# Joining the halves of 32-step inverses: two heads to a 32-row tile instead of four tiles to 64 rows

## The chip, the core and the metric

The kernel runs on one core of a Trainium2 chip. The metric is device time in microseconds (us) of one execution. The engines are TensorE (PE, with PEld for its weight loads), VectorE (DVE), ScalarE (ACT), GpSimd (POOL) and SyncE (SP), which issues every DMA of this kernel. A matrix product reads its two operands from SBUF (`lhsT` is loaded as weights, `rhs` streams past them) and writes PSUM, which here is eight banks of 128 partitions by 512 floats.

## The reference

Four sequences of 768 steps with 8 heads of width 40 carry a 40x40 state through a decayed delta rule; the outputs of the heads, side by side, then go through a normalised two-layer feed-forward network of width 1280 with a residual:

```python
for t in range(S):
    y[:, :, t] = np.einsum('bhd,bhde->bhe', rt, state)
    Sa = np.einsum('bhde,bhe->bhd', state, at)
    state_decay = state * wt[:, :, None, :] - np.einsum('bhd,bhe->bhde', Sa, bt)
    state = state_decay + np.einsum('bhd,bhe->bhde', vt, kt)
...
xn = (x - mu) / np.sqrt(var + 1e-06) * g_ln
ch = np.maximum(xn @ w_ch1, 0.0) @ w_ch2
return (x + ch)
```

Everything is float32.

## The kernel before

**Chunks.** The 768 steps are cut into 24 chunks of C = 32 steps, and the 32 pairs of sequence and head (called heads below) are worked on together. Inside a chunk the rule needs, for each head, the inverse of a 32x32 unit lower triangular matrix made of the decayed keys. The inverse is built from halves of B = 16 steps: with L21 the lower left block of the matrix, W11 and W22 are the inverses of the two diagonal blocks, and the whole inverse has W11 and W22 on its diagonal and W22 L21 W11 below (signs are in L).

**The functions of a chunk.** `prep` (running products of the decays on DVE, scaled operands on POOL, the triangular matrices by the product of L376, from there to DRAM as `d_l`); `invert` (16x16 inverses by elimination, 28 small operations for each slab of two chunks, on DVE for chunks 0 and 1 and on POOL from chunk 2 on; results to DRAM as `d_h`, whose rows hold L21, W11 and the transposed W22 side by side, 16 columns each); `merge`, which this change rewrites; `chain` (the products that need the state: L513, then L523, which multiplies by the joined inverse `tt`, then the new state by L538); `post` (outputs of the chunk: turns L571 and L583, products L598 and L615); `norm` and `moe` (the feed-forward network, once for every two chunks: first layer L786, relu to `hh` on ACT in L789, the rest `hl` on DVE in L791, second layer L770).

**`merge` before.** The 32 heads lie in four groups of eight, two to each half of 64 partitions. Tile `hv` has for each group 32 rows: of these, only the lower 16 are loaded, and constant identities and zeros, written once at the start (L304 to L315), stand around the loaded blocks. Four DMAs a chunk load it, two of them cut into pieces of 16 floats. A product L456 takes `hv` 64 rows by 64 columns against 32 columns (16 of them a chunk: eight for each half), ACT copies the result into `qm` (L458), a second product of the same shape multiplies `qm` with blocks of `hv` (L466), and ACT copies that to `tt` (L468).

**Who sets the order.** Every operation is handed to a planner (`Plan`) with its engine, an estimated duration, a key (about the chunk in which it is due) and what it reads and writes. `Plan.order` plays the whole program through with these estimates and writes out one fixed order for each engine; on the chip each engine runs its list in that order. On PE the planner alternates: products of the recurrence (called sparse here: small tiles) until 2.9 us of them have run, then feed-forward products (dense) for 1.7 us, since it counts instruction records of PE and assumes that 128 of them need 3.8 us to be fetched. PSUM banks 0 to 3 (group A) serve the sparse products, 4 and 5 the first layer, 6 and 7 the second; an operation that opens a bank takes the first that is free in the plan. When the recurrence has ended, the dense products that are left run alone.

Of the kernel before, what the change touches and what calls it, by code (L numbers as in the profile page):

```python
# [16 lines left out]
ALU = mybir.AluOpType  # L17
# [4 lines left out]
C = 32  # L22
B = C // 2
D = 40
# [158 lines left out]
def body(ctx, tc, ea, eb, vr, rd, vt, w1, w1x_in, w2, gl, fe, fd, out):  # L183
    nc = tc.nc
# [27 lines left out]
    start = ring(2, "start", 16, 33)  # L212
# [12 lines left out]
    hv = ring(2, "hv", 8, 9 * B)  # L225
    qm, = ring(1, "qm", 8, 4 * B)
    tt = ring(2, "tt", 8, C)
# [38 lines left out]
    def consts():  # L266
# [21 lines left out]
        op("POOL", 0.3, -84, (), ["qm"], lambda: G.memset(qm, 0.0))  # L288
# [12 lines left out]
        op("ACT", 0.3, -95, (), [("small", 0)], lambda: (A.memzero(small[0]["sd"]), A.sqrt(small[0]["sd"], small[0]["sd"])))  # L301
        for i in range(2):
            j = i + 1
            op("POOL", 0.8, -85 + i, (), two("hv", i, 4), lambda i=i: G.memset(hv[i], 0.0))  # L304

            def f(i=i):
                for q, qs in enumerate(QUADS):
                    up, lo = (ident[qs, 32 * q + B * x:32 * q + B * x + B].unsqueeze(1).broadcast_to([32, 8, B])
                              for x in range(2))
                    at = slice(2 * B * (q % 2), 2 * B * (q % 2) + B)  # L310
                    A.copy(out=hv[i][qs, :, at], in_=lo)
                    A.copy(out=hv[i][qs, :, 6 * B:7 * B], in_=up)
                    if i == 0:
                        A.copy(out=qm[qs, :, at], in_=lo)
            op("ACT", 2.6 if i == 0 else 1.8, -50 + i, ["ident"], two("hv", i, 4) + (["qm"] if i == 0 else []), f)  # L315
# [121 lines left out]
    def merge(c):  # L437
# [3 lines left out]
        for q in range(4):  # L441
            m = 32 * j + 8 * q
            to = hv[i][32 * q + B:32 * q + C]
            to = to[:, :, 3 * B:6 * B] if q % 2 else to.rearrange("a h (x y) -> a h x y", x=3)[:, :, :, B:2 * B]
            of = d_h[s][:, m:m + 8]
            dma(c - 1.3 - soon(c), 55 if q % 2 else 110, [("d_h", s, 0), ("d_h", s, 1)], [("hv", i, q)], to,
                of if q % 2 else of.rearrange("a h (x t) -> a h x t", x=3), 0.5)
        blocks = lambda t, a: t.rearrange("p h (x t) -> p h x t", t=B)[:, :, a:a + 3:2]
        halves = [slice(64 * bb, 64 * bb + 64) for bb in range(2)]
        b = Bank("A")  # L450

        def f(b=b):
# [538 lines left out]
```

## Time and profile before

| what | value |
|---|---|
| three runs | 588.72, 589.93, 594.56 us; median 589.93 |
| the profiled execution | 585.58 us, of it 583.4 us from first to last instruction |
| PE busy | 523.4 us, 90% |
| DVE, ACT, POOL busy | 404.7, 312.3, 279.8 us (69, 54, 48%) |
| the two products of `merge` (L456, L466) | 28.6 and 28.7 us busy, 768 records each |
| the product that uses `tt` (L523) | 20.5 us busy, 1536 records |
| PE granted clock, mean | 0.963 |

A float32 product has two records in the trace, a turn (transpose by the identity) one, a float32r product (feed-forward) one. Records of PE overlap and their ends are modelled, so what a group of products costs is read from its start to the start of the next group, not from the sum of its durations. Some matmuls run at half the granted clock early in the program; from 125 us on it is full.

### The profile page before, as it was taken

The numbers are of one execution on the slowest core, as the hardware profiler recorded it, in microseconds if no ns is written. First come the engines' busy times: TensorE is split into PE (matmuls) and PEld (weight loads), VectorE is DVE, ScalarE is ACT, GpSimd is POOL, SyncE is SP. The second block draws the span as 40 slices with busy tenths as digits, with TensorE's granted clock in tenths as the row PEclk, the third lists the DMA queues.
The fourth block names the chain that finished last, engine by engine and source line by source line (L and its number), as shares of the span: only waits on it lengthen the run. The fifth ranks groups of instructions, "written<-read, shape, count | busy, mean of one in ns | idle before, by whom it ended". The sixth has DMA issues, their size and how long they took to land.

```text
span 583.4 us, 30518 instructions
## 1 busy us (share of the span) xinstructions
PE 523.4 (90%) x13366; PEld 478.0 (82%) x13366; DVE 404.7 (69%) x872; ACT 312.3 (54%) x770; POOL 279.8 (48%) x510
## 2 busy tenths in 40 slices
PE   2528886799999999999999999999999999899995
PEld 2417675699999899998999899999998888799895
DVE  7984977868868668587585774783875648667522
ACT  8536457556555555665555547555746554565221
POOL 9515335575377573753845818637728408000000
PEclk9999558799999999999999999999999999999999
DMA  5374655534444533445444434344452444522000
GB/s 170 76 196 130 180 131 147 145 102 101 118 108 94 134 83 84 128 94 125 109 112 115 107 89 111 92 129 92 106 117 74 92 121 116 126 76 85 5 24 27
DMA packets 103146, 62.32 MB, mean 107 GB/s; under 512 B 82144, under 2 KB 88288, under 8 KB 103008
## 3 DMA queue, kind: packets, MB, share of 16 engines
q1 hardware_dynamic: 103008, 60.32, 41.3%
q8 instruction: 106, 1.74, 1.3%
q14 instruction: 32, 0.26, 0.2%
HBM read 48.49 MB, written 9.44 MB: 99 GB/s over the span
## 4 chain that ended last, share of the span: by engine, by line
PE 82%; DVE 6%; DMA 4%; issue 4%; ACT 2%; POOL 1%; SPq 1%; DVEq 0%; POOLq 0%; ACTq 0%
PE bank L770 20%; PE bank L786 19%; PE bank L466 4%; PE bank L456 4%; PE bank L598 4%; PE bank L376 4%; PE bank L523 3%; PE bank L538 3%; PE bank L615 3%; PE bank L513 3%; PE bank L583 3%; PE bank L488 3%; PE bank L571 2%; PE bank L709 2%; PE bank L398 2%
## 5 line engine op out<-in xcount | busy, mean ns | idle before, releaser
L770 PE MATMUL bank<-w,hh 128*128 128x320 f32 x480 | 114.9, 324 | 0.3 <-issue 0.3
L786 PE MATMUL bank<-xh,w 128*128 128x256 f32 x480 | 107.3, 287 | 1.3 <-issue 0.9
L791 DVE SCALAR_TENSOR_TENSOR hl<-bank,hh 128x256 fp32r<-128x256 f32 x120 | 50.3, 420 | 76.6 <-ACT hh L789 73.8
L789 ACT ACTIVATE hh<-bank 128x256 fp32r<-128x256 f32 x120 | 46.1, 384 | 102.8 <-PE bank L786 100.8
L786 PEld LDWEIGHTS bank<-xh,w 128*128 128x128 f32 x480 | 82.1, 189 | 3.1 <-issue 1.3
L770 PEld LDWEIGHTS bank<-w,hh 128*128 128x128 f32 x480 | 76.4, 188 | 3.4 <-issue 0.4
L770 PE MATMUL bank<-w,hl 128*128 128x320 f32 x240 | 73.8, 307 | 0.0
L359 POOL TENSOR_TENSOR x2s<-wa,qE 40x512 f32<-40x512 f32 x44 | 57.8, 1314 | 23.1 <-DVE qE L347 16.0
L786 PE MATMUL bank<-xl,w 128*128 128x256 f32 x240 | 67.2, 280 | 0.0
L366 POOL TENSOR_TENSOR bk<-bk,gE 104x1024 f32<-104x1024 f32 x22 | 51.5, 2342 | 31.6 <-DMA bk<-in_eb_dram 15.5
L498 POOL MEMSET x5s<- 64x512 f32 x48 | 25.1, 522 | 82.1 <-PE bank L615 66.9
L430 POOL TENSOR_TENSOR yv<-yv,ytmp 64x28 f32<-64x28 f32 (+6 forms) x154 | 53.7, 349 | 12.1
L426 POOL TENSOR_TENSOR ytmp<-yv 64x28 f32<-64x28 f32 (+6 forms) x154 | 51.7, 335 | 11.4
L493 ACT COPY xk<-bank 64x320 f32<-64x320 f32 x96 | 40.2, 419 | 27.4 <-PE bank L488 25.7
L604 DVE TENSOR_TENSOR x5s<-bank,mask 64x256 f32<-64x256 f32 x96 | 40.5, 422 | 14.7 <-PE bank L598 12.2
L786 PEld LDWEIGHTS bank<-xl,w 128*128 128x128 f32 x240 | 45.2, 189 | 0.0
L770 PEld LDWEIGHTS bank<-w,hl 128*128 128x128 f32 x240 | 45.0, 188 | 0.0
L527 ACT COPY x<-bank 32x320 f32<-32x320 f32 x96 | 40.1, 417 | 9.1 <-PE bank L523 7.7
L586 ACT COPY xk<-bank 40x320 f32<-40x320 f32 x96 | 40.2, 418 | 4.4 <-PE bank L583 2.6
L357 POOL MEMSET x2s<- 32x512 f32 x40 | 21.0, 524 | 42.9 <-PE bank L513 25.2
L376 PE MATMUL bank<-x2s,bk 104*64 104x64 f32 x768 | 31.2, 241 | 10.2 <-ACT qc L399 3.3
L456 PE MATMUL bank<-hv 64*64 64x32 f32 x768 | 28.6, 223 | 13.1 <-DMA hv<-d_h 12.6
(133 smaller groups left out, 1144.5 us busy)
## 6 DMA issues: line engine op xcount, KB each, us to landing
wa<-in_ea_dram SPq DMA_DIRECT2D x48, 162.7 KB
bk<-in_eb_dram SPq DMA_DIRECT2D x48, 160.0 KB
vu<-in_vr_dram SPq DMA_DIRECT2D x48, 160.0 KB
wa<-in_ea_dram SPq DMA_DIRECT2D x24, 165.0 KB
x<-in_vt_dram SPq DMA_DIRECT2D x48, 80.0 KB
x5s<-in_rd_dram SPq DMA_DIRECT2D x48, 80.0 KB
out_dram<-ot SPq DMA_DIRECT2D x24, 160.0 KB
r<-in_w_dram SPq DMA_DIRECT2D x10, 320.0 KB
```

The lines of the kernel that those rows point to most:

```text
L359: op(eng, 0.75 * us, kp, W + [("q", i)], [("x2a", x, hf)], lambda hf=hf, rs=rs: e.tensor_tensor(out=x2s[x][rs, hf, 0:512].rearrange("p (h ...
L366: op(eng, 1.25 * us, kp, [("g", i)], K, lambda: e.tensor_tensor(out=kb, in0=kb, in1=g[R, :, 0:C].unsqueeze(2).broadcast_to([104, 16, 2, C] ...
L376: mm(pg[64 * bb:64 * bb + 64, :, h], lhsT=tb[R, 64 * p:64 * p + 64], rhs=x2s[x][R, :, 32 * p:32 * p + 32], start=True, stop=True)
L426: e.tensor_tensor(out=tv, in0=yb[:, :, j + 1:, j:j + 1].broadcast_to(S), in1=yb[:, :, j:j + 1, 0:j].broadcast_to(S), op=ALU.mult)
L430: e.tensor_tensor(out=v, in0=v, in1=tv, op=ALU.add)
L456: mm(po[ps, h], lhsT=hv[i][ps, h, 0:4 * B], rhs=blocks(hv[i], 5)[ps, h], start=True, stop=True)
L493: op("ACT", 0.45, c - 1.2 + 0.1 * bb, [bs[hf]], [X[hf]], lambda b=bs[hf], zs=zs, hf=hf, bb=bb: nc.scalar.copy(out=xk[i][zs, hf, 8 * bb:8 * ...
L604: op("DVE", 0.46, k + 0.5, [b, "mask"], [("z", i)], lambda b=b, zs=zs, ps=ps, hf=hf, bb=bb: nc.vector.tensor_tensor(out=x5s[i][zs, hf, 8 * ...
L770: mm(bank_of(po[u])[:, 0:CH], lhsT=l[:, us], rhs=ws[f"w2_{f // 2}"][:, f % 2, x], start=f == 0 and n == 0, stop=f == 9 and n == 2)
L786: mm(ph, lhsT=l, rhs=r, start=n == 0, stop=n == 7)
L789: yield "ACT", 0.39, [phs[f]], [("hh", f % 2)], lambda f=f: nc.scalar.activation(out=hht[f % 2], in_=bank_of(phs[f])[:, 0:256], func=AF.Re ...
L791: yield "DVE", 0.46, [phs[f], ("hh", f % 2)], [("hl", f % 2)], lambda f=f: nc.vector.scalar_tensor_tensor(out=hlt[f % 2], in0=bank_of(phs[ ...
```

## The change

**The layout.** A 32-row tile now holds two heads: rows 0 to 15 the one, rows 16 to 31 the other, with four such pairs side by side along the columns. `hv` is 128 partitions by 4 by 48, all of it loaded, by one DMA a chunk with 768 bytes to a partition; no constants stand in it.

**The steps of `merge` now.** Two `tensor_scalar` operations write `dg`, in which L21 and W11 of the two heads are spread to block diagonals by a 0/1 column `half`; they run on DVE for chunks 0 and 1 and on POOL from chunk 2 on. The product L452 (16 of 32 rows by 32 columns against 16 columns, on the four diagonal 32x32 tiles) gives the transposed W22 L21; ACT copies it next to a constant identity in `lt` (L455). The product L462 (16 of 32 by 32 against 32 columns) gives W11 and W22 L21 W11; ACT copies it to the left half of `tt` (L465). Four turns (L472) transpose the columns of W11 and W22 for all four groups of partitions at once, 128 rows by 32 columns each, and four ACT operations (L475), one for each group, multiply by `half` and write the right half of `tt`. `chain` reads `tt` with another index. Instead of the constants in `hv` and `qm`, the start writes `ones` and `half` (12 small DVE operations) and the identities of `lt` (two ACT copies).

```diff
-    hv = ring(2, "hv", 8, 9 * B)
-    qm, = ring(1, "qm", 8, 4 * B)
-    tt = ring(2, "tt", 8, C)
+    hv = ring(2, "hv", 4, 3 * B)
+    dg = ring(2, "dg", 2, 4, 2, B)
+    lt = ring(2, "lt", 4, 2 * B)
+    ones, = ring(1, "ones", B)
+    half, = ring(1, "half", 2)
+    tt = ring(2, "tt", 4, 2, C)
...
-        op("POOL", 0.3, -84, (), ["qm"], lambda: G.memset(qm, 0.0))
...
+        def f():
+            for q, qs in enumerate(QUADS):
+                up, lo = (ident[qs, 32 * q + B * x:32 * q + B * x + B] for x in range(2))
+                V.tensor_tensor(out=ones[qs], in0=up, in1=lo, op=ALU.add)
+                for x, t in enumerate((up, lo)):
+                    V.tensor_reduce(out=half[qs, x:x + 1], in_=t, axis=mybir.AxisListType.X, op=ALU.add)
+        op("DVE", 1.5, -60, ["ident"], ["half", "ones"], f)
         for i in range(2):
-            op("POOL", 0.8, -85 + i, (), two("hv", i, 4), lambda i=i: G.memset(hv[i], 0.0))
...
-            op("ACT", 2.6 if i == 0 else 1.8, -50 + i, ["ident"], two("hv", i, 4) + (["qm"] if i == 0 else []), f)
+            op("ACT", 0.3, -50 + i, ["ones"], [("lt", i)], lambda i=i: A.copy(
+                out=lt[i][:, :, 0:B], in_=ones.unsqueeze(1).broadcast_to([128, 4, B])))
...
-        for q in range(4):
...
-            dma(c - 1.3 - soon(c), 55 if q % 2 else 110, [("d_h", s, 0), ("d_h", s, 1)], [("hv", i, q)], to,
-                of if q % 2 else of.rearrange("a h (x t) -> a h x t", x=3), 0.5)
+        dma(c - 1.3 - soon(c), 100, [("d_h", s, 0), ("d_h", s, 1)], [("hv", i)], hv[i],
+            d_h[s][:, 32 * j:32 * j + 32].rearrange("a (g h) n -> g a (h n)", h=4), 0.6)
+        eng, e = ("DVE", nc.vector) if c < 2 else ("POOL", nc.gpsimd)
+        for x in range(2):
+            op(eng, 0.25 if c < 2 else 0.4, c - 0.8 - soon(c), [("hv", i), "half"], [("dg", i)], lambda x=x: e.tensor_scalar(
+                out=dg[i][:, :, :, x].rearrange("p y h t -> p h y t"),
+                in0=hv[i][:, :, 0:2 * B].rearrange("p h (y t) -> p h y t", y=2), scalar1=half[:, x:x + 1], scalar2=None, op0=ALU.mult))
         b = Bank("A")
-            for h in range(8):
-                for ps in halves:
-                    mm(po[ps, h], lhsT=hv[i][ps, h, 0:4 * B], rhs=blocks(hv[i], 5)[ps, h], start=True, stop=True)
-        op("PE", 0.56, km, two("hv", i, 4), [b], f, opens=[b], room=["qm"], recs=32.5)
...
+            for h in range(4):
+                for qs in QUADS:
+                    mm(bank[b.at][qs, B * h:B * h + B], lhsT=dg[i][qs, 0, h].rearrange("p x t -> p (x t)"),
+                       rhs=hv[i][qs, h, 2 * B:3 * B], start=True, stop=True)
+        op("PE", 0.4, km, [("hv", i), ("dg", i)], [b], f, opens=[b], room=[("lt", i)], recs=32.2)
+        op("ACT", 0.27, km, [b], [("lt", i)], lambda b=b: nc.scalar.copy(
+            out=lt[i][:, :, B:2 * B], in_=bank[b.at][:, 0:4 * B].rearrange("p (h t) -> p h t", h=4)))
         b = Bank("A")
...
+                    mm(bank[b.at][qs, C * h:C * h + C], lhsT=lt[i][qs, h], rhs=dg[i][qs, 1, h].rearrange("p x t -> p (x t)"),
+                       start=True, stop=True)
+        op("PE", 0.4, km, [("dg", i), ("lt", i)], [b], f, opens=[b], room=[("tt", i)], recs=32)
...
+        b = Bank("A")
+        def f(b=b):
+            for h in range(4):
+                turn(out=bank[b.at][0:C, 128 * h:128 * h + 128], in_=hv[i][:, h, B:3 * B], identity=ident)
+        op("PE", 0.4, km - 0.1, [("hv", i), "ident"], [b], f, opens=[b], room=[("tt", i)], recs=4)
+        for q, qs in enumerate(QUADS):
+            op("ACT", 0.3, km - 0.1, [b, "half"], [("tt", i)], lambda b=b, q=q, qs=qs: nc.scalar.mul(
+                out=tt[i][qs, :, :, B:C], mul=half[0:C, 1:2],
+                in_=bank[b.at][0:C].rearrange("p (h q x t) -> p h q x t", h=4, q=4, x=2)[:, :, q]))
...
-                    mm(bank[b.at][qs, h * D:h * D + D], lhsT=tt[i][qs, h], rhs=hn[i][qs, h], start=True, stop=True)
+                    mm(bank[b.at][qs, h * D:h * D + D], lhsT=tt[i][qs, h % 4, h // 4], rhs=hn[i][qs, h], start=True, stop=True)
```

**What the planner makes of it, on PE.** The lines of the new program are shifted: L606 is the old L598, L375 the old L376, L778 and L794 the old L770 and L786, L623 the old L615, L496 the old L488. The place is chunk 14 (in the trace of before at 341.8 us). Before:

```order
L456 MATMUL bank_148<-hv_91 64x32 x16
L598 MATMUL bank_149<-x5s_103,vu_107 64x2x32 x16
L466 MATMUL bank_146<-hv_91,qm_93 64x32 x16
L376 MATMUL bank_147<-x2s_99,bk_81 64x2x32 x16
L770 MATMUL bank_152<-w_1_1443,hh_140 128x320 x2
L770 MATMUL bank_152<-w_1_1443,hl_142 128x320
```

And now the same place:

```order
L452 MATMUL bank_153<-hv_91,dg_93 32x16 x16
L606 MATMUL bank_152<-x5s_108,vu_112 64x2x32 x16
L462 MATMUL bank_151<-dg_93,lt_95 32x32 x16
L375 MATMUL bank_154<-x2s_104,bk_81 64x2x32 x16
L778 MATMUL bank_157<-w_2_1539,hh_144 128x320 x2
L778 MATMUL bank_157<-w_2_1539,hl_146 128x320
```

The two products stand between the same neighbours as before. The four turns follow one dense stretch later, ahead of the output product L623:

```order
L794 MATMUL bank_155<-xh_141,w_3_1578 128x256
L794 MATMUL bank_155<-xh_141,w1x 128x256
L794 MATMUL bank_155<-xl_143,w1x 128x256
L472 MATMUL bank_153<-ident,hv_91 32x128 x4
L623 MATMUL bank_151<-xk_110,x5s_108 32x40 x32
L496 MATMUL bank_152<-ident,bk_79 64x40
```

**And on POOL**, where `dg` is new. A slab's elimination ends (`ytmp`, `yv`), zeros and the scaled operands of a later chunk (`x2s`, `bk`) follow. Before, with the slab of chunks 4 and 5:

```order
L426 TENSOR_TENSOR ytmp_90<-yv_89 64x28
L430 TENSOR_TENSOR yv_89<-yv_89,ytmp_90 64x2x14
L498 MEMSET x5s_102 64x512 x2
L357 MEMSET x2s_101 32x512 x2
L359 TENSOR_TENSOR x2s_101<-wa_78,qE_85 40x512 x2
L366 TENSOR_TENSOR bk_80<-bk_80,gE_83 104x1024
L357 MEMSET x2s_98 32x512 x2
L498 MEMSET x5s_103 64x512 x2
```

And now:

```order
L425 TENSOR_TENSOR ytmp_90<-yv_89 64x28
L429 TENSOR_TENSOR yv_89<-yv_89,ytmp_90 64x2x14
L506 MEMSET x5s_107 64x512 x2
L356 MEMSET x2s_106 32x512 x2
L358 TENSOR_TENSOR x2s_106<-wa_78,qE_85 40x512 x2
L365 TENSOR_TENSOR bk_80<-bk_80,gE_83 104x1024
L356 MEMSET x2s_103 32x512 x2
L444 TENSOR_SCALAR dg_93<-hv_91,half_98 128x4x2x16 x2
L444 TENSOR_SCALAR dg_94<-hv_92,half_98 128x4x2x16 x2
L358 TENSOR_TENSOR x2s_103<-wa_77,qE_84 40x512
```

The `dg` of both chunks of a slab stand together, behind the product `bk` of the next slab's second chunk, and wait there for the loads of `hv`.

More of the change, by code (lines that the diff above doesn't have):

```diff
@@ L467, in merge @@
-        op("PE", 0.56, km, two("hv", i, 4) + ["qm"], [b], f, opens=[b], room=[("tt", i)], recs=32)
-        op("ACT", 0.4, km, [b], [("tt", i)], lambda b=b: nc.scalar.copy(
-            out=tt[i], in_=bank[b.at][:, 0:8 * C].rearrange("p (h t) -> p h t", h=8)))
+            for h in range(4):
+                for qs in QUADS:
+                    mm(bank[b.at][qs, C * h:C * h + C], lhsT=lt[i][qs, h], rhs=dg[i][qs, 1, h].rearrange("p x t -> p (x t)"),
+                       start=True, stop=True)
```

26 lines of the change are left out of this document (3 added, 23 removed).

## The prediction

> **What bounds the kernel now.** I read the page's totals and its chain first, then busy time by stretches, then the groups of PE, then PE in order of time.
>
> ```profile
> PE 523.4 (90%) x13366; PEld 478.0 (82%) x13366; DVE 404.7 (69%) x872; ACT 312.3 (54%) x770; POOL 279.8 (48%) x510
> PE 82%; DVE 6%; DMA 4%; issue 4%; ACT 2%; POOL 1%; SPq 1%; DVEq 0%; POOLq 0%; ACTq 0%
> q8 instruction: 106, 1.74, 1.3%
> 0.00:50.00 50.00, 19.95 (x378) 17.05 (x382) 41.41 (x95) 29.16 (x69) 28.03 (x47) 1.00 0.56 148
> 50.00:125.00 75.00, 61.30 (x1309) 51.03 (x1310) 55.12 (x103) 43.77 (x102) 37.12 (x64) 0.73 0.55 142
> 125.00:525.00 400.00, 390.65 (x10952) 360.28 (x10948) 281.13 (x608) 223.69 (x559) 214.69 (x401) 1.00 0.43 106
> ```
>
> The first three rows are totals; the last three are stretches, each with its length, then the busy time of PE, PEld, DVE, ACT and POOL. From 125 to 525 us PE is idle for 400 − 390.65 = 9.35 us. There the recurrence and the feed-forward network share one saturated engine, so a microsecond taken from PE's list is a microsecond of the program, as long as nothing else comes late. Before 125 us PE waits for others.
>
> Now what a piece of PE work costs from its start to the next start. Chunk 14's two products, and the products and turns that I use as prices:
>
> ```profile
> L466 PE MATMUL bank<-hv,qm 64*64 64x32 f32 x768 | 28.7, 226 | 0.8 <-issue 0.8
> L456 PE MATMUL bank<-hv 64*64 64x32 f32 x768 | 28.6, 223 | 13.1 <-DMA hv<-d_h 12.6 <-ACT x L548 0.4
> L523 PE MATMUL bank<-hn,tt 32*32 32x40 f32 x1536 | 20.5, 207 | 0.8 <-ACT tt L468 0.5 <-ACT xk L493 0.3
> 341.04 0.28 PE L786 MATMUL bank<-xh,w1x 128*128 128x256 f32 x1
> 341.16 0.28 PE L786 MATMUL bank<-xl,w1x 128*128 128x256 f32 x1
> 341.37 0.47 PE L583 MATMUL bank<-ident,x 40*40 40x40 f32 x16
> 341.77 1.12 PE L456 MATMUL bank<-hv 64*64 64x32 f32 x32
> 342.82 1.15 PE L598 MATMUL bank<-x5s,vu 104*64 104x64 f32 x32
> 343.90 1.12 PE L466 MATMUL bank<-hv,qm 64*64 64x32 f32 x32
> 344.95 1.15 PE L376 MATMUL bank<-x2s,bk 104*64 104x64 f32 x32
> 353.15 0.79 PE L523 MATMUL bank<-hn,tt 32*32 32x40 f32 x64
> 353.87 0.47 PE L583 MATMUL bank<-ident,x 40*40 40x40 f32 x16
> 355.32 0.55 PE L753 MATMUL bank<-ident,xn 128*128 128x128 f32 x3
> 355.62 0.54 PE L770 MATMUL bank<-w,hh 128*128 128x320 f32 x2
> ```
>
> L456 takes 342.82 − 341.77 = 1.05 us and L466 344.95 − 343.90 = 1.05 us: 32 records each, 33 ns a record. L598 streams twice the columns (64, not 32) and also takes 1.08, so it isn't the streamed columns that set the pace. L523, on 32x32 tiles four abreast, gets 64 records through in 353.87 − 353.15 = 0.72 us, 11 ns a record.
>
> **The change, part by part.**
>
> *Products.* Out go 2.10 us a chunk. L452 and L462 have 16 products, 32 records each, on the same four diagonal 32x32 tiles as L523 and with fewer columns (16 and 32, not 40). Half of 0.72 is 0.36 us. A change of shape may cost a fixed part: the last L786 starts at 341.16, its own pace is 0.12 (341.16 − 341.04), and L583 starts at 341.37, so 0.09 us. If that is in the 0.72, a half is 0.63/2 + 0.09 = 0.41. I take 0.40 for each, with bounds 0.30 (fewer columns help) and 0.41.
>
> *Turns.* Four of 128 rows by 32 columns against 128 streamed. L753 does three of 128 streamed columns in 355.62 − 355.32 = 0.30 us, 0.40 for four. L583 does 16 of 40 columns in 341.77 − 341.37 = 0.40, two abreast, so 50 ns for 40 columns, 0.16 for 128, 0.64 for four that run one after another. I take 0.45, nearer to L753, whose streams have the same length. L583's 16 turns, written to 40 partitions, are 16 records, so a turn with few output columns is a single pass. The Trainium skill, TensorEngine Tiling (Array Packing), section Restrictions, says that column tiling disables the transpose mode for float32; by that each turn would be a two-pass product. An estimate by that rule: eight records at L753's 0.10 are 0.80 us, and the sum would lose 0.35 us a chunk, 7.7 us in all. The trace disagrees with it in those 16 records, and I go by the row.
>
> So a chunk gives 2.10 − 0.40 − 0.40 − 0.45 = **0.85 us** of PE, bounds 2.10 − 0.82 − 0.64 = 0.64 and 2.10 − 0.60 − 0.40 = 1.10. Chunks 4 to 23 lie in the saturated stretch: 20 × 0.85 = 17.0 us. Chunks 2 and 3 lie before 125 us, where PE is busy for 61.30 of 75 us: 2 × 0.85 × 0.82 = 1.4.
>
> *Instruction blocks.* PE's stops come at fixed counts of records:
>
> ```profile
> 56.72 0.94 PE L466 MATMUL bank<-hv,qm 64*64 64x32 f32 x26 [0.82 <-issue]
> 57.59 1.15 PE L598 MATMUL bank<-x5s,vu 104*64 104x64 f32 x32
> 58.68 1.23 PE L523 MATMUL bank<-hn,tt 32*32 32x40 f32 x64
> 59.84 0.39 PE L583 MATMUL bank<-ident,x 40*40 40x40 f32 x6
> 60.46 0.52 PE L583 MATMUL bank<-ident,x 40*40 40x40 f32 x10 [0.23 <-issue]
> ```
>
> 26 + 32 + 64 + 6 = 128 records between two stops, 60.46 − 56.72 = 3.74 us apart; and 13366 records over 106 instruction packets are 126 a packet. So PE cannot run faster than 128 records in some 3.74 us, 29 ns each. In the saturated stretch it now spends 400/10952 = 36.5 ns a record; afterwards, with four records more in each of 20 chunks, (400 − 17)/(10952 + 80) = 34.7. That is still above 29, so the mean doesn't bind, but stretches of small products come nearer to it: the old products, at 33 ns, ran at almost the pace of the blocks, the new ones don't. I charge 2.5 us of further stops (bounds 0 and 6).
>
> *POOL's part.* Two `dg` operations a chunk, 128 elements to a partition each. No POOL row shows this operation; a fill of 32 elements and a two-operand product of 112 bound it:
>
> ```profile
> L418 POOL MEMSET yv<- 64x32 f32 x11 | 1.9, 170 | 28.2 <-issue 11.2 <-DMA yv<-d_l 7.7 <-ACT hh L789 5.7
> L426 POOL TENSOR_TENSOR ytmp<-yv 64x112 f32<-64x112 f32 x22 | 9.0, 410 | 1.7
> 216.99 2.21 POOL L366 TENSOR_TENSOR bk<-bk,gE 104x1024 f32<-104x1024 f32 x1 [1.96 <-DMA bk<-in_eb_dram]
> 220.04 1.36 PE L456 MATMUL bank<-hv 64*64 64x32 f32 x32
> 379.37 2.20 POOL L366 TENSOR_TENSOR bk<-bk,gE 104x1024 f32<-104x1024 f32 x1 [4.83 <-DMA bk<-in_eb_dram]
> 382.57 1.12 PE L456 MATMUL bank<-hv 64*64 64x32 f32 x32
> ```
>
> So 0.17 to about 0.45 us each, 0.4 as I take it, 0.8 for the pair that PE's next product needs. In the saturated stretch they add 20 × 0.8 = 16 us to an engine that is busy for 214.69 of 400, which costs nothing by itself. What counts is when they run: in POOL's list they stand behind the `bk` product. At the two places with least room that product ended at 219.20 and 381.57, and PE reached L456 at 220.04 and 382.57, 0.84 and 1.00 us later. The pair just fits. Behind the waiting `dg` on POOL stand the next chunk's `x2s` and `bk`, which are due later. I charge 1 us (bounds 0 and 4).
>
> *ACT's part.* Two copies of half and a quarter of the old size replace two of 128x256, and four multiplications by a column are new:
>
> ```profile
> L458 ACT COPY qm<-bank 128x256 f32<-128x256 f32 x24 | 8.9, 373 | 8.9 <-PE bank L456 8.7
> L631 ACT ACTIVATE diag<-ident,gt 128x128 f32<-128x128 f32 x2 | 0.7, 395 | 0.0
> ```
>
> With 0.395 for each multiplication and at most 0.373 for a copy, ACT gets at most 4 × 0.395 = 1.58 us a chunk more: 223.69 + 20 × 1.58 = 255 of 383 us, 67%. It stays hidden by the dense products, which PE runs meanwhile. Where the four stand ahead of a relu that PE's next second-layer product needs, that cover is gone; I take nothing, and up to 4 us in the range.
>
> *The load.* One DMA for four takes issue time from SP and cuts `hv` into 128 long pieces instead of 1024 short ones. Only chunk 0 waits for it, so I count it in the start-up.
>
> *Start-up.* Chunk 0 and 1 gain from the shorter products, the single load and 2.7 us less of POOL's fills, and lose by 12 small DVE operations in front of the first scaling chain and by `dg` on a DVE that is still eliminating:
>
> ```profile
> 7.84 0.26 DVE L350 RECIPROCAL last<-qE 104x16 f32<-104x16 f32 x1
> 11.84 3.42 DVE L345 COPY start<-qE 104x16 f32<-104x16 f32 x1
> 13.27 1.91 POOL L290 MEMSET x2s<- 128x1056 f32 x2
> 40.73 2.28 PE L456 MATMUL bank<-hv 64*64 64x32 f32 x32 [12.63 <-DMA hv<-d_h]
> 43.82 1.92 PE L466 MATMUL bank<-hv,qm 64*64 64x32 f32 x32
> ```
>
> Twelve at no more than 0.26 are up to 3.1 us. Against that, the DVE copy of 16 elements that lasted until POOL's fills ended at 15.18 would find them ended earlier, and the two products, 2.28 and 1.92 here, would take about twice 0.40 each at this pace, 2.6 us less. I take the start-up as 0, with ± 3.
>
> **Sum**, against the profiled execution of 585.58 us (span 583.4 and 2.18 around it): −17.0 − 1.4 + 2.5 + 1.0 = −14.9, so 570.7. The median of the three runs is 589.93, 1.0074 times as long, so 570.7 × 1.0074 = **575 us**. With 22 chunks at 0.64 to 1.10 (14.1 to 24.2) and the bounds above, this case alone reaches from 563 to 586.
>
> **Rivals.**
>
> *The blocks take half of it back.* For: the stops 3.74 us apart at 60 us, and sparse stretches that now run at 11 ns a record. Against: 9.35 us of idle time in 400, and dense products between the stretches, which need few records. Stops of 7.5 us more instead of 2.5: 585.58 − 18.4 + 7.5 + 1 = 575.7, or 580 at the median; where all sparse stretches run at the blocks' pace it takes all, 590. I call it 583, nearer to the milder end because of the dense products.
>
> *POOL comes late (slower).* `dg` is now a step between the landing of `hv` and PE's first product, in an in-order list behind a product that itself waited 4.83 us for a DMA at 379 us. If `dg` of each of the ten slabs from chunk 4 on comes later than PE arrives, PE stands, since its list is in order. Half a turn of POOL's cycle, say one `bk` product of 2.2 us and a wait of 0.8, is 3 us a slab: 30 us, 585.6 − 14.9 + 30 = 600.7, or 605. The gain is gone at 1.5 us a slab, and it is slower by 1% at 2.1. For: margins of 0.84 and 1.00. Against: SP's list is shorter, so that `bk` should land earlier, and the second chunk of each slab has its `dg` long before.
>
> *A record costs what it costs (slower).* If the 33 ns of L456 come with issuing two records rather than with the width of the tile, the new products take 1.05 each again, and the turns are on top: 24 × 0.45 = 10.8, so 596.4, or 601. Against it stands L523 with 11 ns a record. The Trainium skill, TensorE: Matmul & The Clock Gate, section "Wait — 56ns, not 53.3ns?", states that start-to-start never drops below about 25 ns however few columns. An estimate by that: 32 × 25 = 0.80 us for each product, no gain but 0.05 a chunk, 589 us. The trace disagrees for tiles abreast (0.72 us for 64).
>
> **How the numbers follow.** Forecast 0.76, blocks 0.12, POOL late 0.09, record cost 0.03. The range of 563 to 588 holds the forecast's own, and the blocks' case; it leaves out the two slower ones and some of the tails, about 0.2. One per cent of 589.93, 5.9 us, is what a measurement of this kernel can tell from no change. Faster by more (under 584): nearly all of the forecast and half of the blocks' case, 0.78. Slower by more (over 595.8): the two slower rivals less a mild form of the first, 0.10. Within: 0.12.
>
> **What would show it.** L452 and L462 at 0.36 to 0.41 us from start to next start, the four turns near 0.45, PE at about 523.4 − 24 × 0.85 = 503 us busy with 13462 records, and a saturated stretch 15 us shorter. Stops marked "issue" of more than 15 us in that stretch would mean the blocks; waits of L452 for POOL's `dg` of 1.5 us and more a slab would mean the second rival. A start-up that ends PE's first `tt` product more than 3 us later would also make me wrong.

## The result, and the profile after

The changed kernel takes 573.99 us (median of four runs, 572.31 to 581.49) against 591.49 us for the kernel before. The ratio is 0.9693, 95% interval 0.9616 to 0.9771. A later timing gave 578.67 against 593.01, ratio 0.9741 (0.9683 to 0.9798). Medians are over all executions; the ratios leave out the slow ones, over 1.5% longer than the fastest of the same kernel. Forecast were 575 us, with a range of 563 to 588. The profiled execution took 572.31 us, 13.3 less than that of before.

First where PE's time went. The page's totals and chain after, then three stretches of the kernel before, then the same of the changed kernel (length, busy time of PE, PEld, DVE, ACT, POOL, granted clock, DMA share, GB/s; the last stretch ends with the span):

```profile
PE 504.1 (88%) x13462; PEld 452.9 (79%) x13462; DVE 404.0 (71%) x888; ACT 333.1 (58%) x848; POOL 304.1 (53%) x551
PE 58%; POOL 9%; issue 5%; DMA 4%; DVE 4%; ACT 3%; SPq 2%; POOLq 0%; DVEq 0%; ACTq 0%
```

```profile
0.00:125.00 125.00, 81.25 (x1679) 68.08 (x1680) 96.52 (x198) 72.93 (x170) 65.15 (x110) 0.84 0.55 144
125.00:530.00 405.00, 395.65 (x11107) 365.06 (x11104) 284.53 (x615) 225.66 (x564) 214.69 (x401) 1.00 0.43 105
530.00:583.40 53.40, 46.46 (x589) 44.83 (x587) 23.65 (x60) 13.70 (x36) 0.00 (x0) 0.98 0.11 34
```

```profile
0.00:125.00 125.00, 81.81 (x1968) 66.18 (x1969) 100.78 (x228) 77.33 (x179) 72.27 (x130) 0.89 0.57 149
125.00:530.00 405.00, 388.77 (x11163) 353.90 (x11163) 289.44 (x624) 248.50 (x651) 231.78 (x422) 0.99 0.41 106
530.00:570.20 40.20, 33.53 (x337) 32.78 (x335) 13.82 (x36) 7.31 (x20) 0.00 (x0) 0.98 0.06 19
```

PE is busy for 523.35 − 504.10 = 19.2 us less. It is idle for 60.0 us before and 66.1 after: 43.8 and 43.2 up to 125 us, 9.4 and 16.2 from there to 530, 6.9 and 6.7 at the end. So 19.2 less work and 6.0 more idle time make the 13.2 us of the span, and all of the new idle time lies in the saturated stretch. A second profile of the changed kernel (span 576.7 us) has PE busy for 505.8 us and idle for 70.9, so this split holds to within some us only. PE's share of the chain of waits falls from 82% to 58%, while POOL's rises from 1 to 9%; the chain after can be followed back only to 87 us, so its shares add up to 85%.

The instructions' own prices, in the changed kernel's list of PE in time, at chunk 14 (start, modelled duration; cost is from start to next start; the last row is cut off by the end of the window):

```profile
335.99 0.47 PE L591 MATMUL bank<-ident,x 40*40 40x40 f32 x16
336.39 0.44 PE L452 MATMUL bank<-hv,dg 32*32 32x16 f32 x32
336.76 1.15 PE L606 MATMUL bank<-x5s,vu 104*64 104x64 f32 x32
337.84 0.45 PE L462 MATMUL bank<-dg,lt 32*32 32x32 f32 x32
338.22 1.15 PE L375 MATMUL bank<-x2s,bk 104*64 104x64 f32 x32
...
341.23 0.60 PE L472 MATMUL bank<-ident,hv 128*32 128x128 f32 x4
341.76 0.44 PE L623 MATMUL bank<-xk,x5s 128*32 128x40 f32 x25
```

L452 costs 0.37 us, L462 0.38, the four turns 0.53; these are also the medians from chunk 4 on. A chunk gives 2.10 − 1.28 = 0.82 us, and 24 × 0.82 = 19.7, close to the busy time that went (19.2 us, and 17.5 by the second profile).

What PE waited for between 125 and 530 us, apart from stops (us in total, times, longest): the kernel before, then the changed one.

```profile
PE bank L753 <- DVE xn L745: 0.4, 1, 0.4
PE bank L786 <- DVE hl L791: 0.4, 1, 0.4
```

```profile
PE bank L794 <- DVE hl L799: 2.0, 2, 1.3
PE bank L452 <- POOL dg L444: 1.5, 2, 1.0
PE bank L531 <- ACT tt L475: 1.1, 1, 1.1
PE bank L623 <- DVE x5s L612: 0.8, 1, 0.8
PE bank L794 <- DVE xl L766: 0.6, 1, 0.6
```

Stops without a releaser, added up along PE's list, are 7.8 us in ten before and 8.6 in eight after. Waits for DVE, POOL and ACT are 1.4 us before and 7.3 after. Two groups of the changed kernel show where two of them come from:

```profile
L444 POOL TENSOR_SCALAR dg<-hv,half 128x128 f32<-128x128 f32 x44 | 29.6, 688 | 22.5 <-DMA hv<-d_h 22.5
L475 ACT ACTIVATE tt<-bank,half 32x128 f32<-32x128 f32 x96 | 34.4, 358 | 10.6 <-PE bank L472 7.5
```

A `dg` on POOL takes 0.69 us in the mean (0.60 in the median), and POOL stands 22.5 us in front of them until `hv` has landed. The longest wait of all, for `hl`, does not come from a new operation. The relu `hh` that `hl` needs stood on ACT behind copies of `yv` and `x`, which the kernel before has too:

```profile
285.46 0.66 ACT L431 COPY yv<-yv 64x256 f32<-64x256 f32 x1 [1.67 <-POOL yv L429]
286.14 0.84 ACT L535 COPY x<-bank 32x320 f32<-32x320 f32 x2
287.91 0.39 PE L794 MATMUL bank<-xh,w 128*128 128x256 f32 x1 [1.27 <-DVE hl L799]
```

ACT had itself just stood 1.67 us for POOL's elimination. The second wait for `hl`, at 410.60 us, came behind DVE's running products of the decays (L346, 2.45 us) and a copy.

Last, the end of the recurrence: the last records of its last product in the kernel before, and that product in the changed one:

```profile
541.86 0.48 PE L615 MATMUL bank<-xk,x5s 104*32 104x40 f32 x28 [0.19 <-DVE x5s L604]
```

```profile
533.83 0.80 PE L623 MATMUL bank<-xk,x5s 128*32 128x40 f32 x64
```

It ends at 534.6 us instead of 542.3, 7.7 us earlier. The rest of the gain is what comes after: 570.2 − 534.6 = 35.6 us are left instead of 41.1, with 221 records instead of 269, since more of the dense products ran beside the recurrence.

### The profile page after: what moved, and what is told of

Same layout as the page of the kernel before. It is cut to its first block, busy times and chain, and to the rows that moved or that the text cites. A ratio compares the mean times of both kernels' runs of the same rounds, so it can differ in the third digit from the quotient of the medians.

```text
span 570.2 us, 30783 instructions
## 1 busy us (share of the span) xinstructions
PE 504.1 (88%) x13462; PEld 452.9 (79%) x13462; DVE 404.0 (71%) x888; ACT 333.1 (58%) x848; POOL 304.1 (53%) x551
## 4 chain that ended last, share of the span: by engine, by line
PE 58%; POOL 9%; issue 5%; DMA 4%; DVE 4%; ACT 3%; SPq 2%; POOLq 0%; DVEq 0%; ACTq 0%
PE bank L778 16%; PE bank L794 16%; POOL ytmp L425 3%; POOL yv L429 3%; PE bank L606 3%; PE bank L375 3%; PE bank L496 2%; PE bank L546 2%; PE bank L623 2%; PE bank L531 2%; PE bank L521 2%; PE bank L591 2%; PE bank L579 2%; SPq L266 1%; PE bank L472 1%
## 5 line engine op out<-in xcount | busy, mean ns | idle before, releaser
L778 PE MATMUL bank<-w,hh 128*128 128x320 f32 x480 | 116.5, 328 | 0.0
L794 PE MATMUL bank<-xh,w 128*128 128x256 f32 x480 | 107.9, 288 | 2.6 <-DVE hl L799 2.0
L794 PEld LDWEIGHTS bank<-xh,w 128*128 128x128 f32 x480 | 82.8, 190 | 4.3 <-DVE hl L799 2.4
L778 PEld LDWEIGHTS bank<-w,hh 128*128 128x128 f32 x480 | 76.6, 189 | 3.4
L778 PE MATMUL bank<-w,hl 128*128 128x320 f32 x240 | 74.6, 311 | 0.0
L794 PE MATMUL bank<-xl,w 128*128 128x256 f32 x240 | 67.6, 282 | 0.0
L358 POOL TENSOR_TENSOR x2s<-wa,qE 40x512 f32<-40x512 f32 x44 | 52.9, 1202 | 23.8 <-DVE qE L346 17.1
L425 POOL TENSOR_TENSOR ytmp<-yv 64x28 f32<-64x28 f32 (+6 forms) x154 | 55.5, 360 | 11.3
L501 ACT COPY xk<-bank 64x320 f32<-64x320 f32 x96 | 40.2, 419 | 17.7 <-PE bank L496 15.7
L794 PEld LDWEIGHTS bank<-xl,w 128*128 128x128 f32 x240 | 45.8, 191 | 0.0
L778 PEld LDWEIGHTS bank<-w,hl 128*128 128x128 f32 x240 | 45.6, 190 | 0.0
L444 POOL TENSOR_SCALAR dg<-hv,half 128x128 f32<-128x128 f32 x44 | 29.6, 688 | 22.5 <-DMA hv<-d_h 22.5
L375 PE MATMUL bank<-x2s,bk 104*64 104x64 f32 x768 | 31.1, 240 | 11.4 <-issue 5.4
L475 ACT ACTIVATE tt<-bank,half 32x128 f32<-32x128 f32 x96 | 34.4, 358 | 10.6 <-PE bank L472 7.5
```

What stands on the lines that cost most here:

```text
L358: op(eng, 0.75 * us, kp, W + [("q", i)], [("x2a", x, hf)], lambda hf=hf, rs=rs: e.tensor_tensor(out=x2s[x][rs, hf, 0:512].rearrange("p (h ...
L375: mm(pg[64 * bb:64 * bb + 64, :, h], lhsT=tb[R, 64 * p:64 * p + 64], rhs=x2s[x][R, :, 32 * p:32 * p + 32], start=True, stop=True)
L425: e.tensor_tensor(out=tv, in0=yb[:, :, j + 1:, j:j + 1].broadcast_to(S), in1=yb[:, :, j:j + 1, 0:j].broadcast_to(S), op=ALU.mult)
L501: op("ACT", 0.45, c - 1.2 + 0.1 * bb, [bs[hf]], [X[hf]], lambda b=bs[hf], zs=zs, hf=hf, bb=bb: nc.scalar.copy(out=xk[i][zs, hf, 8 * bb:8 * ...
L778: mm(bank_of(po[u])[:, 0:CH], lhsT=l[:, us], rhs=ws[f"w2_{f // 2}"][:, f % 2, x], start=f == 0 and n == 0, stop=f == 9 and n == 2)
L794: mm(ph, lhsT=l, rhs=r, start=n == 0, stop=n == 7)
```

## The experiments

The runs come from three chips. On the first (the products twice, one 32-row tile at a time, no turns, the kernel before with other prices) the kernel before took 590.05 us, on the second (one 64-row tile at a time, turns as products, five prices, `dg` on ACT) 591.0, on the third (the other four) 593.01. The runs are compared by their ratios to it: the changed kernel has 0.9693 and, on the third chip, 0.9741. One per cent is 5.9 us.

**1. The products twice: is PE's time the program's time?** In both products:

```diff
-            for h in range(4):
+            for h in (0, 1, 2, 3) * 2:
                 for qs in QUADS:
```

> The changed kernel, with the 32 records of L452 and of L462 each issued twice into the same bank; order, planner prices and results as in the changed kernel. Theory A (PE is the bound, and a record on four tiles abreast costs what the changed profile shows, 0.37 and 0.38 us for 32): the second pass costs 0.28 to 0.37 us each, the smaller figure if a change of shape is in the first, so 20 saturated chunks x 0.56 to 0.74 = 11 to 15 us more: 585 to 589 us against 574. Theory B (instruction blocks: 128 records in no less than 3.74 us, 29 ns a record): 64 records x 29 ns = 1.87 us a chunk, 37 us more: 611. Theory C (after the change other engines are the bound, PE is only 58% of the chain of waits): most of it is hidden, less than 5 us more: under 579.

604.08 us, ratio 1.0291 (1.0191 to 1.0390): 30 us more by the medians, 32 to 35 by the two ratios of the changed kernel. That is more than twice what theory A gave, and the 37 of theory B lie within the intervals, so the list has to tell them apart. PE's list at chunk 12, then the largest waits:

```profile
311.00 0.73 PE L452 MATMUL bank<-hv,dg 32*32 32x16 f32 x64
311.71 1.15 PE L606 MATMUL bank<-x5s,vu 104*64 104x64 f32 x32
```

```profile
PE bank L531 <- issue: 5.7, 5, 1.7
PE bank L462 <- issue: 3.2, 3, 1.7
PE bank L496 <- issue: 3.0, 2, 1.6
```

The price itself is as theory A had it: in the median over the chunks 64 records cost 0.67 and 0.68 us (0.71 in the row shown), so the second pass costs 0.30, 9 to 10 ns a record, and some 0.08 us of the first pass is the change of shape. PE is busy for 522.0 us, 17.9 more. But the stops grow from 8.6 us in eight to 18.6 in 21 (counted to 545 us, since this program is longer), and idle time as a whole by 9.9 us. So stops take their part when 64 records a chunk are added, about 10 us; 29 ns for each record would be 37. That PE no longer binds (theory C) is refuted.

**2. One tile at a time: what makes a record cheap?** The two loops exchanged, in the changed kernel and then in the kernel before.

```diff
-            for h in range(4):
-                for qs in QUADS:
+            for qs in QUADS:
+                for h in range(4):
```

> The changed kernel, with the two loops of both products exchanged: the four heads of one 32-row tile run one after another before the next tile, instead of the four tiles in turn. Same 32 records, same shapes, same results, same order of everything else. Theory A (the pace comes from tiles that work abreast; one tile alone takes 46 ns a record, 0.72 us over 16 records on each tile of L531, or 66 ns, as in the old 64-row products with two tiles abreast): each product takes 32 x 46 to 66 ns = 1.5 to 2.1 us instead of 0.37, so 20 chunks x 2 x 1.1 to 1.7 = 44 to 68 us more: 618 to 642. Theory B (a narrow tile makes a record cheap, in whatever turn): no change, 574 within 3.

> The kernel before with the two loops of both old products exchanged: the eight heads of one 64-row tile one after another, then the other tile, instead of the two in turn. Same records, same results, same order of all else. Theory A (a 64-row tile alone takes 66 ns a record and two abreast halve that): each product takes 2.1 us instead of 1.05, 22 chunks x 2 x 1.05 = 46 us more: 636 against 590. Theory B (33 ns is what a record on a 64-row tile costs, alone or not): no change, 590 within 3. Theory C (a record on one tile alone costs 25 ns whatever its height, as the run with one 32-row tile at a time showed with 0.81 us for 32): faster, 0.8 us each, 22 x 2 x 0.25 = 11 us less: 579.

The changed kernel with one 32-row tile at a time: 595.43 us, ratio 1.0121 (1.0053 to 1.0190). The kernel before with one 64-row tile at a time: 621.6, ratio 1.0509 (1.0406 to 1.0613). Their lists:

```profile
304.72 0.88 PE L452 MATMUL bank<-hv,dg 32*32 32x16 f32 x32
305.53 1.15 PE L606 MATMUL bank<-x5s,vu 104*64 104x64 f32 x32
306.61 0.89 PE L462 MATMUL bank<-dg,lt 32*32 32x32 f32 x32
307.43 1.15 PE L375 MATMUL bank<-x2s,bk 104*64 104x64 f32 x32
```

```profile
317.87 1.84 PE L456 MATMUL bank<-hv 64*64 64x32 f32 x32
319.64 1.15 PE L376 MATMUL bank<-x2s,bk 104*64 104x64 f32 x32
```

With the times of the unaltered kernels this makes a table of what a record costs:

| tile | one at a time | in turn |
|---|---|---|
| 64 by 64 | 1.77/32 = 55 ns | two tiles: 33 ns |
| 32 by 32 | 0.81/32 = 25 ns | four tiles: 12 ns, 9 to 10 without the change of shape |

Both halves of the layout count: the narrow tile alone is worth 55 to 25, and its being one of four that work in turn 25 to 12. For the 32-row tile theory A was right in kind and wrong in size (0.81 and 0.82 us, not 1.5 to 2.1); for the 64-row tile theory A came near (1.77, not 2.1), and B and C fell. The times follow the prices: 24 × 2 × 0.44 = 21 us against 23.6 more of busy time and a ratio about 4% higher, and 24 × 2 × 0.72 = 34.6 against 35.0 of busy time and 30 us. The Trainium skill, TensorE: Matmul & The Clock Gate, section "Wait — 56ns, not 53.3ns?", gives about 25 ns as the least from start to start; one tile alone agrees (25), tiles in turn do not (9 to 12). One record in this table is one of two passes of a float32 product.

**3. The turns: what do they cost, and are they one pass?** Left out with the multiplications that carry them; and written as products.

```diff
-                turn(out=bank[b.at][0:C, 128 * h:128 * h + 128], in_=hv[i][:, h, B:3 * B], identity=ident)
+                pass
```

> The changed kernel without the four turns of a chunk (L472) and without the four multiplications by a column that carry them (L475): the right half of tt is filled with zeros once at the start, so W22 is left out of the result; the order of all else is held. Theory A (PE is the bound): 0.53 us a chunk go, 20 x 0.53 = 10.6 us, and 1.1 us of waiting for tt: 562 to 564 against 574. Theory B (the multiplications on ACT cost more than the turns on PE, because relus queue behind them): 15 us or more go, under 559. Theory C (PE is no longer the bound): less than 5 go, over 569.

```diff
-                turn(out=bank[b.at][0:C, 128 * h:128 * h + 128], in_=hv[i][:, h, B:3 * B], identity=ident)
+                mm(bank[b.at][0:C, 128 * h:128 * h + 128], lhsT=hv[i][:, h, B:3 * B], rhs=ident, start=True, stop=True)
```

> The changed kernel with its four turns a chunk written as plain float32 products with the identity, in the same tiles of 128 rows by 32 columns; same results, same order. Theory A (a turn in such a tile is a single pass, a product two passes): eight records instead of four, (0.53 - 0.08)/4 = 0.11 us each, 0.08 + 8 x 0.11 = 0.96 us instead of 0.53, 20 x 0.43 = 9 us more: 583 against 574. Theory B (in a column tile a turn costs what a product costs): the same time, 574 within 3.

Left out: 567.27 us, ratio 0.9589 (0.9497 to 0.9681), which is 6 to 9 us less than the changed kernel by its two ratios. That lies between theories A and C, and the intervals overlap, so it only says that the turns and all that hangs on them cost some 6 to 9 us. The 15 of theory B are at the edge of what the intervals allow.

As products: 581.08 us, ratio 0.9792 (0.9706 to 0.9877), 3 to 6 us more. In its list L472 has eight records, and takes 0.99 us from start to next start where nothing is mixed into it, 0.46 more than the turns:

```profile
312.94 0.95 PE L472 MATMUL bank<-ident,hv 128*32 128x128 f32 x7
313.63 0.27 PE L623 MATMUL bank<-xk,x5s 128*32 128x40 f32 x6
313.73 0.27 PE L472 MATMUL bank<-ident,hv 128*32 128x128 f32 x1
```

Theory A had 0.96. The 20 × 0.46 = 9 us are not all seen in the time; the intervals leave room for them. So a turn in a tile of 128 rows by 32 columns is a single pass. The rule of the Trainium skill that column tiling disables the transpose mode for float32 (TensorEngine Tiling (Array Packing), section Restrictions) does not show here: the turns have four records, and a product has twice as many at almost twice the time.

**4. The order alone.** The two kernels with other planner prices and the same instructions. In the kernel before the old products and their copies got the prices that the change gives to its own; in the changed kernel all five of its prices were set to what its trace showed (with `dg` on DVE, in chunks 0 and 1, from 0.25 to 0.3), and then only PE's three. One line of each edit:

```diff
-        op("PE", 0.56, km, two("hv", i, 4), [b], f, opens=[b], room=["qm"], recs=32.5)
+        op("PE", 0.4, km, two("hv", i, 4), [b], f, opens=[b], room=["qm"], recs=32.5)
```

```diff
-        op("PE", 0.4, km - 0.1, [("hv", i), "ident"], [b], f, opens=[b], room=[("tt", i)], recs=4)
+        op("PE", 0.53, km - 0.1, [("hv", i), "ident"], [b], f, opens=[b], room=[("tt", i)], recs=4)
```

> The kernel before with nothing changed but four numbers of its planner: the two old products are planned at 0.40 us instead of 0.56, their copies at 0.27 and 0.30 instead of 0.40, as the change plans its own. Same instructions and results, another order: on SP the load of yv for the slab of chunks 2 and 3 stands ahead of the load of bk again, behind which it waited until 82.03 us in the profile of before. Theory A (the gain is the price of the instructions; the order is worth nothing): 591 within 3. Theory B (the 7 us that the changed kernel is ahead at 125 us come from the order of the start-up): 584 to 588. A slower time, over 595, would mean that prices told too low spoil the order.

> The changed kernel with only the planner's prices set to what its trace showed: dg on POOL 0.6 us instead of 0.4, the products 0.37 and 0.38, the turns 0.53 instead of 0.4, the four multiplications 0.36 instead of 0.3. Same instructions and results, another order. Theory A (the 7 us of idle time that PE has more than before, from 125 us on, come from prices told too low): 3 to 6 us less, 568 to 571 against 574. Theory B (order is worth little, as the old kernel with other prices showed: 2.4 us): 574 within 3. Over 580 would mean that the order is chance.

> The changed kernel with only PE's three planner prices set to what its trace showed (0.37, 0.38 and 0.53 us), those of POOL and ACT as in the changed kernel. With all five set it took 583 us, with stops of 17.3 us instead of 8.6, most of them behind L623, L496 and L531 in a row. Theory A (PE's prices set how the planner mixes small products with dense ones, and its mixture was lucky before): 581 to 585 again. Theory B (POOL's and ACT's prices did it): 574 within 3.

The kernel before with other prices: 587.41 us (10 runs), ratio 0.9959 (0.9917 to 1.0002). Its elimination for chunks 2 and 3 on POOL starts 9 us earlier than before and as early as in the changed kernel. The first fill of it, in the kernel before, the changed one, and this one:

```profile
85.60 0.15 POOL L418 MEMSET yv<- 64x32 f32 x1 [2.98 <-ACT w L701]
```

```profile
77.22 0.15 POOL L417 MEMSET yv<- 64x32 f32 x1
```

```profile
76.59 0.15 POOL L418 MEMSET yv<- 64x32 f32 x1
```

And yet the ratio says 2.4 us, and 5 at the most. The recurrence's lead at chunk 2 (the product of `tt` starts 7.9 us earlier here, 10.5 in the changed kernel) is order and not the price of an instruction. Here it melts away in the saturated stretch: at chunk 23 the product of `tt` starts 1.0 us later than before. In the changed kernel the lead stays, 9.3 us at chunk 4 and 8.0 at chunk 23; what PE saves in between goes into dense products. The 2.6 us by the medians fit theory A (within 3 of the kernel before) better than B: that lead alone is not the gain.

The changed kernel with five prices from its trace: 583.2 us, ratio 0.9882 (0.9817 to 0.9946). With PE's three alone: 568.13, ratio 0.9588 (0.9528 to 0.9647). The same instructions, 15 us apart by the medians and 17 by the ratios, with the changed kernel between them. No theory of these two runs held: truer prices for all five made it 8 to 11 us slower, not faster, truer prices for PE alone made it faster, and the order is worth much more than the 2.4 us of the old kernel had suggested; the case named last, that over 580 the order is chance, is what came. What the five prices did is seen in PE's waits between 125 and 530 us, and at one of the places:

```profile
PE bank L531 <- issue: 6.9, 3, 3.0
PE bank L778 <- issue: 3.5, 4, 1.7
PE bank L452 <- issue: 2.8, 3, 1.1
PE bank L462 <- issue: 2.3, 1, 2.3
```

```profile
412.80 0.48 PE L496 MATMUL bank<-ident,bk 40*64 40x40 f32 x16
413.20 0.69 PE L531 MATMUL bank<-hn,tt 32*32 32x40 f32 x50
415.72 0.34 PE L531 MATMUL bank<-hn,tt 32*32 32x40 f32 x14 [1.84 <-issue]
```

There 130 records (64 of L623, 16 of L496, 50 of L531) went through in 1.8 us, and PE then stood for 1.84. Such rows of small products stand together more often in that order: 13 stops with 17.3 us, against eight with 8.6. The order by PE's three prices is fast for another reason: it has 11 stops with 11.1 us, more than the changed kernel, but PE waits for ACT only 1.8 us and for DVE and POOL not at all, against 10.5 for the three in the changed kernel on the same chip. So an order moves both, stops and waits. Which of the other prices (`dg` on POOL and DVE, ACT's 0.36) turned the first of these orders that way was not tried apart.

**5. `dg` on ACT, and the mixture.** The changed kernel with `dg` on ACT; again beside the changed kernel itself; and with dense products put earlier.

```diff
-            op(eng, 0.25 if c < 2 else 0.4, c - 0.8 - soon(c), [("hv", i), "half"], [("dg", i)], lambda x=x: e.tensor_scalar(
+            op("ACT", 0.36, c - 0.8 - soon(c), [("hv", i), "half"], [("dg", i)], lambda x=x: nc.scalar.mul(
```

```diff
-    SPARSE, DENSE = 2.9, 1.7
+    SPARSE, DENSE = 2.2, 1.7
```

> The changed kernel with the two dg operations of every chunk on ACT as multiplications by a column (planned at 0.36 us each), instead of on POOL (on DVE for chunks 0 and 1); same results, the planner orders anew. In the changed kernel POOL took 0.60 us for a dg and stood 22.5 us in front of them, waiting for hv. Theory A (dg on POOL is what makes PE wait: 1.5 us for dg, 1 for bk behind it, part of the rest): 2 to 4 us less, 570 to 572 against 574. Theory B (the same standing before hv moves to ACT, where relus queue behind it, 2 us a slab): 10 x 2 = 20 us more, 594. Theory C: it lands on idle time, 574 within 2.

> The changed kernel, unaltered, on the chip of the next three runs, so that they are compared with it and not only with the kernel before. Expected: ratio 0.965 to 0.975 to the kernel before, as at first (0.9693).

> The kernel of the run with dg on ACT, unaltered, beside the changed kernel on one chip. Theory A (dg on ACT is better: POOL's 30 us of dg and its 22 us of standing before hv are gone, PE busy 500.2 us and fewer long waits): 4 to 6 us less than the changed kernel. Theory B (the 0.9617 against 0.9693 was scatter): within 2 us of it.

> The kernel with dg on ACT, and the planner told to put a dense product after 2.2 us of small ones instead of 2.9; same instructions and results. Theory A (the stops come where small products of 128 records stand together for less than 3.74 us, so that an earlier dense product saves most of the 9.2 us of stops): 4 to 7 us less than with 2.9, 561 to 564. Theory B (each dense product that is put earlier makes the recurrence later, and other engines' waits grow by as much): within 3 of it, or slower.

With `dg` on ACT: 567.84 us, ratio 0.9617 (0.9532 to 0.9703); again 570.9, ratio 0.9620 (0.9562 to 0.9678), beside 578.67 and 0.9741 (0.9683 to 0.9798) for the changed kernel on the same chip, within the 0.965 to 0.975 expected. The group of `dg` in the first of these runs:

```profile
L444 ACT ACTIVATE dg<-hv,half 128x128 f32<-128x128 f32 x48 | 17.2, 397 | 2.4 <-DMA hv<-d_h 2.2
```

One costs 0.40 us on ACT against 0.60 on POOL, and ACT stands 2 us in front of them, where POOL stood 22.5: theory B, that the standing would move along, is refuted. In the second pair of profiles PE waits 0.4 us for `dg` in the saturated stretch, against 2.7 in the changed kernel. It beats both kernels: by 4 us against the changed one in the first pair of ratios, where the intervals overlap, and by 7 on the same chip, where they don't, which is theory A's side in both runs. How much of the 7 us is `dg` and how much is a luckier order stays open, after experiment 4.

With dense products after 2.2 us: 570.69 us, ratio 0.9612 (0.9545 to 0.9678), the same as with 2.9. The stops fell from 9.7 us in 16 to 5.4 in nine, and PE's waits for ACT and DVE rose from 5.6 to 7.5. Theory B: the mixture trades the one for the other.

## Why the prediction was right

**PE is the bound: right.** Busy time fell by 19.2 us, time by 13.3. Doubled products cost their price and more, and products slowed by exchanged loops cost theirs (experiments 1 and 2). In seven profiles of kernels with the same PE instructions, in this order or another, PE is busy for 499.4 to 506.9 us, so the fall of 19.2 is known to within 3 to 5 us.

**The products: right.** 0.40 each was taken, 0.37 and 0.38 came. The reading of L523, 11 ns a record on four tiles, carried over to other columns, and the fixed part of 0.09 for a change of shape measures 0.08. That a narrow tile and tiles in turn both count could not be seen in the rows of before.

**The turns: mis-sized, in the bounds.** 0.45 taken, 0.53 measured, between L753's 0.40 and L583's 0.64. It takes 0.08 × 20 = 1.6 us from the sum, which the two products give back (0.05 × 20 = 1.0). The net per chunk is 0.82 against 0.85.

**Instruction blocks: charged 2.5, measured 0.9 more (7.8 to 8.6 us).** Stops do come at a count: in PE's list of the changed kernel they lie 1275, 1783, 381, 1147, 3055, 892 and 382 records apart, all multiples of 127 to 128. But 3.74 us for such a block was no limit. Part of it ran at a granted clock of 0.5 (that of 58.8 to 89.5 us; L523 takes 1.16 us in it and 0.72 at chunk 14), and in the saturated stretch of the changed kernel 128 records and the stop behind them took from 2.2 to 4.9 us. Whether the stops cost 5, 9 or 17 us is set by how the planner's order happens to pack small products, not by the mean of ns a record from which I charged. The rival with the blocks did not happen in this order, but it did for the same instructions in another (583.2 us, with 9.5 us more stops than before; the rival had 7.5 and 583).

**POOL: the price missed its bounds, the consequence came near.** I bounded a `dg` by 0.17 and 0.45; it takes 0.60. The pair in front of L452 is 1.2 us, not 0.8, and more than the margins of 0.84 and 1.00. It made PE wait for only 1.5 us in all, twice, in the slabs of chunks 4 and 8, where I had charged 1. At the second of them POOL stood before `hv`, and not behind `bk`:

```profile
213.79 3.35 POOL L444 TENSOR_SCALAR dg<-hv,half 128x128 f32<-128x128 f32 x4 [3.23 <-DMA hv<-d_h]
```

So the margins were measured against the wrong event: in nine of the ten slabs from chunk 4 on, the load sets when `dg` can start. The second rival needed 1.5 us a slab, and got 1.5 in ten.

**ACT and DVE: charged 0, measured 3.9 us more than before.** The waits for `tt`, `hl`, `x5s` and `xl` in the list above are the term that was mis-sized: ACT's new work was put down as hidden by the dense products, with up to 4 us in the range, and DVE had no term. Only the 1.1 us for `tt` are a wait for the new operations themselves; the two for `hl` came behind work that the kernel before has too. What brought that work into PE's way, the new order or the new work on ACT and POOL, is not shown. ACT is busy for 58% and DVE for 71% of the span, but each runs its list in order, and a busy share says nothing of when a result is due. The new idle time of the saturated stretch, 6.9 us, is 0.9 of stops, 1.5 for `dg`, 0.6 for `bk`, which ran at 441.14 us behind an elimination on POOL, and these 3.9; charged were 2.5, 1 for POOL and 0. In the second profile the waits for POOL are 2.7 us and those for ACT and DVE 7.8.

**The load: wrong as it was put.** "Only chunk 0 waits for it" held for the kernel before. Now POOL waits for it ahead of nearly every slab's `dg`, 22.5 us in all; it reaches PE only through the second of the two waits above, 0.5 us.

**Start-up: right in the sum, not in its parts.** Idle time up to 125 us changed by 0.6 us, within 0 ± 3, and the first product of `tt` starts at 45.21 instead of 46.21. What I did not foresee is that the order brings chunks 2 and 3 forward by 10.5 and 7.9 us; in experiment 4 such a lead of 7.9 us was worth 2.4 us at the end.

**What would show it.** Prices, busy time (504.1 against 503) and records came as named. "A saturated stretch 15 us shorter" did not: the recurrence ends 7.7 us earlier, and 5.5 come from the shorter tail. PE's work can be saved in one place and cashed in another.

**Record cost: refuted.** 12 ns a record, not 33. With one tile at a time it is 25, and the time 595 us, near that rival's 601.

**What was luck.** The forecast took the planner's order as given. The same instructions take 568, 574 to 579 and 583 us in three orders; by the ratios 0.9588 to 0.9882 the change is worth 24 us in one and 7 in another. So the agreement with 575 is closer than the argument had a right to. Two errors in the sum also partly offset each other: 19.2 us of PE's work went where 18.4 were forecast, and 6.0 us of idle time came where 3.5 were charged. What a chunk saves on PE is shown, 0.82 us, and that PE's time for these products is the program's; how much of the gain is the order's is open. The range was not added up evenly either: its lower end takes the 3 us of start-up, its upper end neither these nor ACT's 4, and with all bounds it would reach 593. The measured time is far from both ends.

## What to carry to other kernels

Where an engine is saturated, price an edit from one group's start to the next group's start in the list of that engine, and look for a row with the same tile shape and the same turn-taking between tiles, since both set the pace of small products. Then count the idle time apart from the work: engines that were hidden come into view as soon as the bound gets shorter, an engine that is busy for 58% among them. With a planner that writes the order from estimated prices, time the same instructions in two or three orders before a change of one or two per cent is put down to an instruction; better estimates do not have to give a better order.

## What the runs showed that I had not expected

- A 64 by 64 tile alone takes 55 ns a record, a 32 by 32 tile alone 25, four of these in turn 9 to 12 (experiments 1 and 2).
- A multiplication by a column, 128 partitions by 128 elements, takes 0.60 us on POOL in the median and up to 1.64; on ACT 0.40. On DVE, in the start-up, four took from 0.29 to 1.85.
- Stops of PE without a releaser come at a count of records, not at a time: where 128 of them had run in 2 us or less, PE then stood for 0.5 to 2.3 us.
- The same program's PE work differs by run, with the half clock falling on other instructions: along PE's list the dense products take about 239 us in the first profile of the changed kernel and 243 in the second, the preparation of the weights 20.5 and 17.7; the spans are 570.2 and 576.7 us.
